# Half-width maximum products in an attention loop: one of three maxima per key tile made of 256 keys in each row half of TensorE, both in one PSUM bank

## The chip, the cores and the metric

The kernel runs on one core of a Trainium2 chip. Its engines are TensorE (PE, with its weight loads as PEld), VectorE (DVE), ScalarE (ACT), GpSimd (POOL) and SyncE (SP, which issues most DMAs). Each engine has its own instruction stream; semaphores order them. The metric is the device time of one execution in microseconds (us), as a median of several runs.

## The reference

One transformer block over 2048 tokens of width 640: attention with 32 heads of width 20, then a gated feed-forward network (FFN) of width 1728, each with a residual and a layer norm ahead of it.

```
h  = x + softmax(q k^T / sqrt(20)) v @ wo     (q, k, v from layernorm(x) @ wqkv)
h2 = h + (silu(z @ w_gate) * (z @ w_up)) @ w_down     (z = layernorm(h))
```

The softmax is exact in the sense that the row maximum is subtracted before the exponential. For each query the kernel therefore needs the maximum of its 2048 scores before the exponentials of that query begin.

## The kernel before, in words

**Stages.** First come the layer norm and the projections to queries, keys and values, beside which the first row maxima are found (`max_four`, L230). Then comes the attention loop (L1375). Then the output projection and the FFN follow.

**Units and key tiles.** The 32 heads are 8 groups of 4 heads. A unit `u` is one group with one chunk of 512 queries, so there are `NU` = 32 units. A unit is worked in `NT` = 16 key tiles of 128 keys, 512 key tiles in all. For one key tile the loop issues:

- four score products (`scores`, L1295), one for each head: 128 keys against 512 queries into one PSUM bank, followed by the exponential on ScalarE (L1306) from that bank to `probs`;
- one weighing of the key tile two earlier (`weigh`, L1308): four products with `values`, one for each head, each on 32 columns of TensorE, all 128 rows. The operands are plain fp32, and the trace shows each as two passes, eight matmuls in all;
- three maximum products for units that come later (`max_one`, L268): 128 queries against 512 keys into one bank, followed by a maximum over the 512 on VectorE (L280) into one slot of the small tile `mx` of that unit;
- and small pieces: a part of the preparation of FFN weights, loads of queries, the output of finished units (`row_sums` L1318, with one copy on ScalarE for each unit, L1320).

**Row halves.** The contraction of a score or maximum product has 60 or 62 rows only, so TensorE holds two of them at once: rows 0 to 63 (`b` = 0) serve two of the four heads and rows 64 to 127 (`b` = 1) the other two. Below, a small letter is a product in half 0, a capital one in half 1.

**Order.** It is written by hand. `ORDER` (L41) has one string for even and one for odd key tiles; `W` is the weighing with the small pieces, `s` and `S` are scores, `m` and `M` are maximum products:

```
ORDER = ("WsSmmSsM", "WSsMMsSm")
```

So one half gets four products of 512 columns and the other three, in turn. `singles` holds the list of maximum products for each half, and `next_max` (L1356) takes the next one of a half. When all maxima of a unit are there, `max_all` (L284) takes the maximum over its slots, and `max_parts`, `max_turn`, `max_load` or `max_finish` put the negated maximum into two extra rows of that unit's queries. There are 1472 such products of one half and 512 keys; at three a tile they last for some 491 of the 512 tiles, after which the order is `sSsSW`.

**PSUM.** Of the eight banks, four go round the scores (`ps_one`, L952), three go round the maximum products (`ps_max`, L959), and one holds the weighing's sum (`acc`). A product whose bank is still being read waits at its weight load.

Of the kernel before, what the change touches and what calls it, by code (L numbers as in the profile page):

```python
# [9 lines left out]
F32 = mybir.dt.float32  # L10
# [4 lines left out]
ALU = mybir.AluOpType  # L15
AX = mybir.AxisListType

P = 128
S = 2048
D = 640  # L20
H = 32
# [4 lines left out]
CH = 512  # L26
NC = S // CH
TPC = CH // P
# [9 lines left out]
LOWEST = -3.4028234e38  # L38
GD = G * DH

ORDER = ("WsSmmSsM", "WSsMMsSm")  # L41


@with_exitstack
def tile_block(ctx: ExitStack, tc: tile.TileContext, x, wqkv, wo, wg, wu, wd, out):
    nc = tc.nc
# [100 lines left out]
    NU = NG * NC  # L147
# [4 lines left out]
    stk = att_ctx.enter_context(tc.tile_pool(name="stk", bufs=1, side="right"))  # L152
    k_stk = [stay.tile([P, 2, S], F32R, name="k_stk0", tag="first")]
    v_stk = [stay.tile([P, NT, VG], F32, name="v_stk0", tag="second")]
    keys, queries, values = {}, {}, {}
# [24 lines left out]
    def load_keys(g, cs):  # L180

        k = keys[g] = k_stk[g % 2]
        stack(k[:, :, cs], 1, g, cs.start // CH)
# [11 lines left out]
        )  # L195

    def mx_tile(u, **tag):
        return stk.tile([P, 2, 2, TPC, NC], F32, name=f"mx{u}", **tag)

    mxs = {u: mx_tile(u) for u in range(NU) if u % NC < 2 or u == 2}  # L200

# [63 lines left out]

        return differences, maxima

    def max_one(u, kc, t, pair, b):  # L268

        ps = ps_max()  # L270
        if u not in mxs:
            mxs[u] = mx_tile(u, tag="mx_late", bufs=3)
        rows = slice(b * ROW, b * ROW + NPART)
        nc.tensor.matmul(  # L274
            ps,
            queries[u][rows, pair, t * P : (t + 1) * P],
            keys[u // NC][rows, pair, kc * CH : (kc + 1) * CH],
            start=True, stop=True,
        )
        nc.vector.tensor_reduce(  # L280
            mxs[u][:, b, pair, t, kc : kc + 1], ps, axis=AX.X, op=ALU.max
        )

    def max_all(u):  # L284

        ends[u] = stk.tile([P, G * TPC], F32, name="neg", tag="neg", bufs=2)
        nc.vector.tensor_reduce(
            ends[u], mxs[u].rearrange("p b h t k -> p (b h t) k"), axis=AX.X, op=ALU.max, negate=True
        )

    def max_parts(u):

        neg = ends[u]
        both = ends[u] = stk.tile([P, 2, G * TPC], F32R, name="neg2", bufs=2)
        nc.gpsimd.tensor_copy(both[:, 0], neg)
        nc.gpsimd.tensor_tensor(
            out=both[:, 1], in0=neg, in1=both[:, 0].bitcast(F32), op=ALU.subtract
        )
# [66 lines left out]
    with tc.tile_pool(name="pa", bufs=2) as pa:  # L365
# [21 lines left out]
        slot = [0]  # L387
# [468 lines left out]
        for c in range(NC):  # L856
# [7 lines left out]
            for j, (kind, *which) in enumerate(work):  # L864
# [31 lines left out]
                else:  # L896
# [10 lines left out]
                    def ps_max():  # L907
                        n = turn[0] % 5
                        turn[0] += 1
                        if n > 2:  # L910
                            return psum_two.tile([P, CH], F32, name="ps_max", tag="ps_two")
                        return psum.tile([P, CH], F32, name="ps_max", tag="ps_max", bufs=3)
# [4 lines left out]
                if (c, j) in ((1, 14), (1, 16), (2, 4), (3, 4)):  # L917
                    n = c if c > 1 else (j - 14) // 2
# [376 lines left out]
    def scores(u, kt, j, probs):  # L1295

        p, b = divmod(j, 2)
        rows = slice(b * ROW, b * ROW + NPART + 2)
        ps = ps_one()
        nc.tensor.matmul(  # L1300
            ps,
            keys[u // NC][rows, p, kt * P : (kt + 1) * P],
            queries[u][rows, p, :],
            start=True, stop=True,
        )
        nc.scalar.activation(probs[p][:, b, :], ps, AF.Exp, scale=scale)  # L1306
# [43 lines left out]
            )  # L1350

    todo, tail, accs, later, full, now = [], [], {}, {}, [], [0]
    singles = [[(*a, b) for a in rest] for b in range(2)]
    left = {u: sum(2 for a in rest if a[0] == u) for u in range(1, NU)}

    def next_max(b):  # L1356
        if singles[b]:
            a = singles[b].pop(0)
            max_one(*a)
            left[a[0]] -= 1  # L1360
            if left[a[0]] == 0:
                full.append(a[0])

    def weigh_next():
        u, kt, probs = todo.pop(0)
        if kt == 0:
            accs[u] = psum.tile([P, CH], F32, name="acc", tag=f"ps_{last % 3}")
        weigh(u, kt, probs, accs[u])
        if kt == NT - 1:
            queues = [nc.sync] if u + 1 < NU else [nc.scalar, nc.sync]  # L1370
            tail.append((u, *row_sums(accs.pop(u), *queues)))

    extra = []
    preparing = prepare_weights()
    for u in range(NU):  # L1375
        g, c = divmod(u, NC)
        if g == NG - 1 and c >= 2:
            _, first, ln, flips, _ = ahead
            extra = [*first, *ln, lambda: None, *flips]
        for kt in range(NT):  # L1380
            now[0] = u * NT + kt
            probs = [pp.tile([P, 2, CH], F32, name="probs") for _ in range(2)]
            heads = [[0, 2], [1, 3]]
            order = ORDER[now[0] % 2] if singles[0] or singles[1] else "sSsSW"
            for op in order:
                if op in "mM":
                    next_max(int(op == "M"))
                elif op in "sS":
                    scores(u, kt, heads[op == "S"].pop(0), probs)
                else:  # L1390
                    if len(todo) == 2:
                        weigh_next()
                    for f in later.pop(now[0], ()):
                        f()
                    if extra:
                        extra.pop(0)()
                    if preparing and u and kt not in (3, 4):
                        preparing.pop(0)()
                    if now[0] == (NU - NC) * NT + 8:
                        unit_ring, last_ring = weight_rings()  # L1400
                        unit_ring.fill()
# [51 lines left out]
    u, o, r = tail.pop()  # L1453
# [561 lines left out]
```

## Time and profile before

| what | value |
|---|---|
| median of 3 runs | 2027.66 us (2025.42 to 2028.07) |
| the profiled execution, its own time | 2025.84 us |
| its span, first to last instruction | 2024.0 us |
| granted TensorE clock, mean | 0.999 |
| first and last score product start | 319.2 and 1455.2 us |
| first and last maximum (L280) start | 321.2 and 1391.6 us |

The profile is of one execution. Busy time of an engine counts its instructions from their recorded start to their recorded end; on TensorE and ScalarE one instruction's end overlaps the next one's start, so the distance from start to start says what one costs in a stream, and the recorded duration says when its result is there. The line numbers are those of the kernel before. A weight load on PEld is listed with the line of its matmul.

### The profile page before, as it was taken

How to read it: one execution, taken by the hardware profiler on the slowest of the kernel's cores; microseconds unless marked ns; L12 is line 12 of the kernel's file. 1: busy time of each engine (PE TensorE's matmuls, PEld its weight loads, DVE VectorE, ACT ScalarE, POOL GpSimd, SP SyncE). 2: the span in 40 equal slices, each digit the busy share in tenths (PEclk: the TensorE clock that was granted, in tenths of full speed). 3: DMA queues.
4: the chain of work that ended last, by engine and by line, in shares of the span. 5: the costliest groups of instructions: out<-in, count | busy, mean ns of one | idle time of the engine just before them, and what ended most of it. 6: DMA issues, size and time to landing. Idle time of an engine off the chain costs nothing. (4 is left out here: it accounts for less than half of the span.)

```text
span 2024.0 us, 39916 instructions
## 1 busy us (share of the span) xinstructions
PE 2003.7 (99%) x14302; PEld 1242.0 (61%) x14302; DVE 1602.4 (79%) x2816; ACT 1439.9 (71%) x2827; POOL 788.5 (39%) x1166
## 2 busy tenths in 40 slices
PE   8999999999999999999999999999999999999999
PEld 6999995333334333333333333345588888888888
DVE  5687778888888898988988988875387666676677
ACT  4678878999999999999999999987633222212221
POOL 7464423334443453443400011011155444744555
PEclk9999999999999999999999999999999999999999
DMA  7877563443634544435412132221258654974642
GB/s 245 255 254 261 180 207 83 117 146 95 189 104 139 153 143 128 155 128 173 148 58 68 36 85 58 80 63 56 59 182 296 218 189 154 353 268 159 204 150 95
DMA packets 199340, 310.35 MB, mean 153 GB/s; under 512 B 53744, under 2 KB 87856, under 8 KB 198120
## 3 DMA queue, kind: packets, MB, share of 16 engines
q1 hardware_dynamic: 192552, 284.21, 43.7%
q0 software_dynamic: 6496, 23.60, 3.9%
q8 instruction: 114, 1.87, 0.4%
q14 instruction: 82, 0.67, 0.1%
q10 hardware_dynamic: 96, 0.00, 0.0%
HBM read 208.11 MB, written 99.19 MB: 152 GB/s over the span
## 5 line engine op out<-in xcount | busy, mean ns | idle before, releaser
L1306 ACT ACTIVATE probs<-ps_one 128x512 f32<-128x512 f32 x2048 | 1056.6, 615 | 61.2 <-PE ps_one L1300 35.3
L280 DVE TENSOR_REDUCE mx<-ps_max 128x1 f32<-128x512 f32 x1472 | 924.9, 684 | 106.3 <-PE ps_one L1300 77.6
L1300 PE MATMUL ps_one<-q_stk,k_stk 62*128 62x512 f32 x2048 | 583.3, 450 | 0.7 <-DMA q_stk<-m_d 0.6
L1310 PE MATMUL acc<-probs,v_stk 128*32 128x512 f32 x4096 | 546.2, 606 | 0.0
L1300 PEld LDWEIGHTS ps_one<-q_stk,k_stk 62*128 62x128 f32 x2048 | 248.7, 184 | 441.2 <-ACT probs L1306 416.7
L274 PE MATMUL ps_max<-k_stk,q_stk 60*128 60x512 f32 x1472 | 374.9, 426 | 1.0 <-DVE mx L261 0.9
L274 PEld LDWEIGHTS ps_max<-k_stk,q_stk 60*128 60x128 f32 x1472 | 272.8, 186 | 26.9 <-DVE mx L280 2.1
L1693 DVE TENSOR_TENSOR tmp<-ps_a,tmp 128x512 f32<-128x512 f32 x208 | 141.2, 689 | 122.4 <-PE ps_a L1478 96.7
L261 DVE TENSOR_REDUCE mx<-ps_max 128x2 f32<-128x512 f32 x288 | 180.7, 685 | 63.9 <-PE ps_max L239 58.7
L1310 PEld LDWEIGHTS acc<-probs,v_stk 128*32 128x32 f32 x4096 | 80.6, 108 | 179.0 <-issue 168.0
L251 ACT ACTIVATE ps_max<-ps_max 128x512 f32<-128x512 f32 x288 | 151.6, 584 | 42.9 <-PE ps_max L239 40.3
L1572 PE MATMUL ps_b<-halves,yp 128*128 128x320 f32 x1032 | 179.0, 308 | 1.5 <-DMA halves<-j_d 1.2
L1572 PEld LDWEIGHTS ps_b<-halves,yp 128*128 128x128 f32 x1032 | 165.2, 188 | 17.5 <-POOL yp L90 1.5
L1478 PE MATMUL ps_a<-t,units 128*128 128x512 f32 x624 | 162.5, 396 | 0.0
L90 POOL TENSOR_TENSOR yp<-y,yp 128x256 fp32r<-128x256 f32 x96 | 60.2, 627 | 189.8 <-ACT yp L89 189.8
L1478 PE MATMUL ps_a<-z,units 128*128 128x512 f32 x516 | 133.9, 394 | 0.0
L1478 PEld LDWEIGHTS ps_a<-t,units 128*128 128x128 f32 x624 | 112.6, 188 | 18.5
L1345 POOL TENSOR_TENSOR o<-o,rb 128x512 f32<-128x512 f32 x31 | 39.9, 1286 | 199.1 <-DMA q_stk<-q_d 74.1
L1577 DVE TENSOR_TENSOR h<-ps_b,h 128x320 f32<-128x320 f32 x248 | 109.9, 480 | 6.9 <-PE ps_b L1572 5.4
L643 PE MATMUL ps_one<-z_hi,w_lo 64*128 64x512 f32 x380 | 113.5, 392 | 0.0
L643 PE MATMUL ps_one<-z_lo,w_hi 64*128 64x512 f32 x380 | 112.3, 392 | 0.0
L643 PE MATMUL ps_one<-z_hi,w_hi 64*128 64x512 f32 x380 | 111.7, 393 | 0.0
(225 smaller groups left out, 2637.4 us busy)
## 6 DMA issues: line engine op xcount, KB each, us to landing
units<-w_d SPq DMA_DIRECT2D x186, 256.0 KB
w_d<-stage SPq DMA_DIRECT2D x106, 256.0 KB
halves<-j_d SPq DMA_DIRECT2D x70, 320.0 KB
j_d<-stage SPq DMA_DIRECT2D x42, 320.0 KB
k_stk<-k_d SPq DMA_DIRECT2D x64, 160.0 KB
q_stk<-q_d SPq DMA_DIRECT2D x64, 160.0 KB
raw<-k_d SPq DMA_DIRECT2D x62, 160.0 KB
raw<-q_d SPq DMA_DIRECT2D x54, 160.0 KB
```

Source lines behind the costliest of these rows:

```text
L251: nc.scalar.activation(ps, ps, AF.Relu)
L261: nc.vector.tensor_reduce(mx[:, b, :, t, kc], ps.rearrange("p (j n) -> p j n", j=2), axis=AX.X, op=ALU.max,)
L274: nc.tensor.matmul(ps, queries[u][rows, pair, t * P : (t + 1) * P], keys[u // NC][rows, pair, kc * CH : (kc + 1) * CH], start=True, stop=True,
L280: nc.vector.tensor_reduce(mxs[u][:, b, pair, t, kc : kc + 1], ps, axis=AX.X, op=ALU.max)
L643: nc.tensor.matmul(ps, a[rows], b[rows], start=(i == n == 0), stop=(i == 1 and n == last), skip_group_check=True,)
L1300: nc.tensor.matmul(ps, keys[u // NC][rows, p, kt * P : (kt + 1) * P], queries[u][rows, p, :], start=True, stop=True,)
L1306: nc.scalar.activation(probs[p][:, b, :], ps, AF.Exp, scale=scale)
L1310: nc.tensor.matmul(acc[32 * j : 32 * j + 32, :], values[u // NC][:, kt, j * VW : j * VW + 32], probs[j // 2][:, j % 2, :], start=(kt == 0) ...
L1478: nc.tensor.matmul(ps.rearrange("p (t n) -> p t n", t=TPC), w[k][:, i], z[k][:, :, j], start=(first and m == 0), stop=(last and m == len(n ...
L1572: nc.tensor.matmul(ps, a, b, start=(n == 0), stop=(n == len(pairs) - 1))
L1577: nc.vector.tensor_tensor(out=h, in0=ps, in1=h, op=ALU.add)
L1693: add = lambda out, ps, x: nc.vector.tensor_tensor(out=out, in0=ps, in1=x, op=ALU.add)
```

## The change

The three maximum products of a key tile are divided in another way. Each tile now has one in half 0 (`m`), one in half 1 (`M`), and one that is made of two products of 256 keys, one in each half (`h` and `H`), which write the two halves of one bank. One maximum on VectorE then reads that bank and writes two values, the maxima of two heads over the same 256 keys. Every key tile has the same order. The two halves of the array may not write one bank at the same time, so ahead of `H` stands a no-operation on TensorE that touches the bank and thereby waits for `h`.

Two such tiles cover the 512 keys of both heads, so the list of work (`rest`) is used up at the same rate as before. A maximum over 256 keys for the second part needs a slot of its own: `mx` gets two more slots, filled with the lowest number in advance (on GpSimd for tiles that exist from the start, on VectorE for the late ones), and `max_all` reduces over six slots where it reduced over four.

```diff
-ORDER = ("WsSmmSsM", "WSsMMsSm")
+ORDER, LAST_ORDER = "WhSmsSHMs", "sSsSW"
...
     def mx_tile(u, **tag):
-        return stk.tile([P, 2, 2, TPC, NC], F32, name=f"mx{u}", **tag)
+        n = NC + (2 if tag else u > 0)
+        return stk.tile([P, 2, 2, TPC, n], F32, name=f"mx{u}", **tag)
...
+    def max_slots(u):
+
+        if u not in mxs:
+            mxs[u] = mx_tile(u, tag="mx_late", bufs=3)
+            nc.vector.memset(mxs[u][:, :, :, :, NC:], LOWEST)
+        return mxs[u]
...
+    def max_half(ps, i, u, kc, t, pair, b):
+
+        k0 = kc * CH + i * (CH // 2)
+        cols = slice(b * CH // 2, (b + 1) * CH // 2)
+        max_product(ps[:, cols], u, t, pair, b, k0, k0 + CH // 2)
+
+    def max_halves(ps, i, u, kc, t, pair):
+
+        slot = kc
+        if i:
+            n = halved[u, t, pair] = halved.get((u, t, pair), 0) + 1
+            slot = NC - 1 + n
+            assert slot < max_slots(u).shape[-1]
         nc.vector.tensor_reduce(
-            mxs[u][:, b, pair, t, kc : kc + 1], ps, axis=AX.X, op=ALU.max
+            max_slots(u)[:, :, pair, t, slot], ps.rearrange("p (j n) -> p j n", j=2),
+            axis=AX.X, op=ALU.max,
         )
...
     def next_max(b):
-        if singles[b]:
-            a = singles[b].pop(0)
+        if not whole and rest:
+            a = rest.pop(0)
+            whole.extend((*a, i) for i in (b, 1 - b))
+        if whole:
+            a = whole.pop(0)
             max_one(*a)
-            left[a[0]] -= 1
-            if left[a[0]] == 0:
-                full.append(a[0])
+            counted(a[0], 1)
+
+    def next_half(b):
+
+        if not halves_of and rest:
+            a = rest.pop(0)
+            halves_of.extend((i, a, []) for i in range(2))
+        if not halves_of:
+            return
+        i, a, banks = halves_of[0]
+        if not banks:
+            banks.append(ps_max())
+            max_half(banks[0], i, *a, b)
+        else:
+            nc.tensor.keepalive_nop([nc.tensor.lower_ap(banks[0])])
+            max_half(banks[0], i, *a, b)
+            max_halves(banks[0], i, *a)
+            counted(a[0], 2 * i)
+            halves_of.pop(0)
...
+    for u in range(1, NU):
+        if u in mxs:
+            nc.gpsimd.memset(mxs[u][:, :, :, :, NC:], LOWEST)
...
-            order = ORDER[now[0] % 2] if singles[0] or singles[1] else "sSsSW"
-            for op in order:
+            for op in ORDER if rest or whole or halves_of else LAST_ORDER:
                 if op in "mM":
                     next_max(int(op == "M"))
+                elif op in "hH":
+                    next_half(int(op == "H"))
```

`max_product` holds the matmul that `max_one` had. The stages ahead of the attention loop and behind it are as they were.

More of the change, by code (lines that the diff above doesn't have):

```diff
@@ L266, in max_four, with max_product @@
         return differences, maxima
[L268 to L272, printed above, removed]
+    def max_product(ps, u, t, pair, b, k0, k1):
         rows = slice(b * ROW, b * ROW + NPART)
@@ L276, in max_one @@
             queries[u][rows, pair, t * P : (t + 1) * P],
-            keys[u // NC][rows, pair, kc * CH : (kc + 1) * CH],
-            start=True, stop=True,
-        )
+            keys[u // NC][rows, pair, k0:k1],
+            start=True, stop=True, skip_group_check=True,
+        )
+    halved = {}
+    def max_slots(u):
[3 more added lines that the diff above has]
+        return mxs[u]
+    def max_one(u, kc, t, pair, b):
+        ps, mx = ps_max(), max_slots(u)
+        max_product(ps, u, t, pair, b, kc * CH, (kc + 1) * CH)
+        nc.vector.tensor_reduce(mx[:, b, pair, t, kc : kc + 1], ps, axis=AX.X, op=ALU.max)
+    def max_half(ps, i, u, kc, t, pair, b):
[8 more added lines that the diff above has]
+            assert slot < max_slots(u).shape[-1]
         nc.vector.tensor_reduce(
-            mxs[u][:, b, pair, t, kc : kc + 1], ps, axis=AX.X, op=ALU.max
+            max_slots(u)[:, :, pair, t, slot], ps.rearrange("p (j n) -> p j n", j=2),
+            axis=AX.X, op=ALU.max,
         )
@@ L1352, in tile_block, with counted @@
     todo, tail, accs, later, full, now = [], [], {}, {}, [], [0]
-    singles = [[(*a, b) for a in rest] for b in range(2)]
     left = {u: sum(2 for a in rest if a[0] == u) for u in range(1, NU)}
-    def next_max(b):
-        if singles[b]:
-            a = singles[b].pop(0)
-            max_one(*a)
-            left[a[0]] -= 1
-            if left[a[0]] == 0:
-                full.append(a[0])
+    whole, halves_of = [], []
+    def counted(u, n):
+        left[u] -= n
+        if n and left[u] == 0:
+            full.append(u)
+    def next_max(b):
+        if not whole and rest:
[3 more added lines that the diff above has]
+            a = whole.pop(0)
+            max_one(*a)
+            counted(a[0], 1)
[15 more added lines that the diff above has]
+            halves_of.pop(0)
     def weigh_next():
```

## The prediction, on record before the changed kernel ran

> **What bounds the kernel now.** I read the busy shares first, then the windows of the attention loop, then single key tiles in the timeline.
>
> ```profile
> PE 2003.7 (99%) x14302; PEld 1242.0 (61%) x14302; DVE 1602.4 (79%) x2816; ACT 1439.9 (71%) x2827; POOL 788.5 (39%) x1166
> 400.00:600.00 200.00, 200.00 (x1408) 78.37 (x1405) 179.30 (x301) 194.78 (x383) 86.95 (x163) 1.00 0.43 133
> 1000.00:1200.00 200.00, 200.00 (x1407) 78.11 (x1404) 179.41 (x300) 195.11 (x383) 19.43 (x28) 1.00 0.21 59
> PEld ps_one L1300 <- ACT probs L1306: 416.7, 529, 1.6
> ```
>
> The window columns are PE, PEld, DVE, ACT and POOL, then the clock. PE is busy all the time, ACT 97%, DVE 90%; the wait list even says that score weights wait for the exponential. Busy shares do not decide between PE and ACT here, because recorded durations overlap. Starts do. Two key tiles on PE, and ACT in three places:
>
> ```profile
> 901.09 1.06 PE L1310 MATMUL acc<-probs,v_stk 128*32 128x512 f32 x8
> 902.09 0.50 PE L1300 MATMUL ps_one<-q_stk,k_stk 62*128 62x512 f32 x2
> 902.43 0.39 PE L274 MATMUL ps_max<-k_stk,q_stk 60*128 60x512 f32 x1
> 902.43 0.39 PE L1300 MATMUL ps_one<-q_stk,k_stk 62*128 62x512 f32 x1
> 902.66 0.51 PE L274 MATMUL ps_max<-k_stk,q_stk 60*128 60x512 f32 x2
> 902.89 0.40 PE L1300 MATMUL ps_one<-q_stk,k_stk 62*128 62x512 f32 x1
> 904.22 0.50 PE L1300 MATMUL ps_one<-q_stk,k_stk 62*128 62x512 f32 x2
> 904.55 0.39 PE L274 MATMUL ps_max<-k_stk,q_stk 60*128 60x512 f32 x1
> 904.56 0.39 PE L1300 MATMUL ps_one<-q_stk,k_stk 62*128 62x512 f32 x1
> 904.78 0.51 PE L274 MATMUL ps_max<-k_stk,q_stk 60*128 60x512 f32 x2
> 905.02 0.40 PE L1300 MATMUL ps_one<-q_stk,k_stk 62*128 62x512 f32 x1
> 905.34 1.06 PE L1310 MATMUL acc<-probs,v_stk 128*32 128x512 f32 x8
> 906.34 0.50 PE L1300 MATMUL ps_one<-q_stk,k_stk 62*128 62x512 f32 x2
> 902.62 0.60 ACT L1306 ACTIVATE probs<-ps_one 128x512 f32<-128x512 f32 x1
> 904.07 0.62 ACT L1306 ACTIVATE probs<-ps_one 128x512 f32<-128x512 f32 x1
> 905.50 0.66 ACT L1306 ACTIVATE probs<-ps_one 128x512 f32<-128x512 f32 x1
> 907.41 0.71 ACT L1306 ACTIVATE probs<-ps_one 128x512 f32<-128x512 f32 x1
> ```
>
> A tile takes 2.13 us (902.09 to 904.22). On PE it is a closed chain of starts. The weighing to the first score pair is 1.00 (901.09 to 902.09, and 905.34 to 906.34). That pair costs 0.34, since its weights load with nothing beside them. Two slots of 0.23 follow. The last product to the next weighing is 0.32 (905.02 to 905.34). The sum is 1.00 + 0.34 + 0.23 + 0.23 + 0.32 = 2.12, the tile but for rounding. ACT has room: from 905.50 to 907.41 lie four steps of an unbroken run, 0.48 each, so four exponentials need 1.91. PE bounds the loop.
>
> The last of the four slots shows what is wasted. One score product stands alone there, with half of the array idle, because one half has four products and the other three.
>
> The rows also show that **the halves run ahead of each other**. Written as `sSmmSsM` (or its mirror), a strict order would give: a score pair, one maximum product alone, the second maximum product with a score, a score with the third maximum product. The trace has, behind the pair, a maximum product with a score (902.43), two maximum products together (x2 at 902.66, and again at 904.78) and a score alone. So the score written behind the second maximum product started ahead of it, and the product written last started ahead of the score before it. Each half takes its own products as they come.
>
> **The change, part by part.**
>
> *The slots.* Half 0 now gets `h m s s`, half 1 gets `S S H M`: three and a half products of 512 columns each, where it was four against three.
>
> ```profile
> 303.66 0.39 PE L643 MATMUL ps_one<-z_hi,w_hi 64*128 64x512 f32 x1
> 303.88 0.51 PE L239 MATMUL ps_max<-raw 60*128 60x256 f32 x4
> 304.13 0.39 PE L643 MATMUL ps_one<-z_hi,w_hi 64*128 64x512 f32 x1
> L239 PE MATMUL ps_max<-raw,raw 60*128 60x256 f32 x608 | 81.1, 287 | 0.2
> ```
>
> In the stage before, four products of 256 columns in row halves, two in each half, take 0.25 us (303.88 to 304.13): 0.12 each in a half, with weights. So in half 0 of the new tile `h` ends at 0.23 (0.34 less 0.23, plus 0.12), then come three products of 0.23, the last one from 0.69. In half 1 the scores run to 0.57, `H` to 0.69 and `M` from there. The weighing starts 0.32 later, at 1.01, where it was at 1.13. **PE alone: 2.13 - 0.12 = 2.01 us**, with 490.7 tiles (1472 / 3) some 57 us.
>
> *The added matmul and weight load* are inside the 0.12. *The maximum* keeps its price: two outputs from 512 inputs cost VectorE what one does.
>
> ```profile
> L280 DVE TENSOR_REDUCE mx<-ps_max 128x1 f32<-128x512 f32 x1472 | 924.9, 684 | 106.3 <-PE ps_one L1300 77.6
> L261 DVE TENSOR_REDUCE mx<-ps_max 128x2 f32<-128x512 f32 x288 | 180.7, 685 | 63.9 <-PE ps_max L239 58.7
> 902.85 1.89 DVE L280 TENSOR_REDUCE mx<-ps_max 128x1 f32<-128x512 f32 x3 [0.24 <-PE ps_one L1300]
> ```
>
> Three in a run take 1.89, or 0.60 a step and 1.81 a tile: under 2.01, so DVE is not the bound. Its banks are held longer, though. `h` takes one of three banks at the tile's start. By these steps the maxima start at 0.66 (`m`: 0.23 + 0.39 + 0.04), 1.27 (`H`) and 1.87 (`M`, done at 2.55). The next `h` needs `H`'s bank at 2.0, free at 1.95; the next `M` loads its weights at 2.6, free at 2.6. Nothing is left over, so each late maximum is paid by PE.
>
> *The wait on itself.* The trace has no such wait. What is queued behind it: `H`, `M`, the last score and the next weighing, and with them ScalarE's fourth exponential and two maxima. `h` starts with the tile; as a first product it ends at 0.11 + 0.28 = 0.39.
>
> ```profile
> 905.98 0.67 ACT L1306 ACTIVATE probs<-ps_one 128x512 f32<-128x512 f32 x1
> 906.70 0.18 PEld L1300 LDWEIGHTS ps_one<-q_stk,k_stk 62*128 62x128 f32 x1
> L274 PEldq EVENT_SEMAPHORE  x66: 51/51/320, 365.0 to 1324.9; - x66
> ```
>
> From an awaited end (905.98 + 0.67 = 906.65) to the weights behind it is 0.05; a separate wait instruction on PE's queue lasts 0.05 when it is already met. So the wait passes at 0.44 to 0.49, `H`'s weights take 0.11, and `H` could start at 0.55 to 0.60 where its half is free at 0.57. Lower end: nothing, hidden under `S`. Upper end: the wait covers everything issued before it, and 0.33 us a tile is lost (below). I take nothing, the value that the rows give.
>
> *What is late next.* Four banks go round the scores, so the fourth score needs the fourth exponential of the tile before.
>
> ```profile
> 904.54 0.63 ACT L1320 ACTIVATE o<-acc 128x512 f32<-128x512 f32 x1
> 908.62 0.73 PE L1300 MATMUL ps_one<-q_stk,k_stk 62*128 62x512 f32 x3
> ```
>
> That exponential ends 2.60 us after its tile's start (904.07 + 0.62 - 902.09). Add 0.05 for the wait, 0.11 for weights, 0.32 to the weighing and 1.00 to the next pair: 4.08 us for two tiles, so **a tile can't be under 2.04**. That is above PE's 2.01, and I take it: 2.13 - 2.04 = 0.09 less a tile, 490.7 x 0.09 = 44 us.
>
> With the slack gone, the copy that ScalarE makes once a unit (0.48 in a run) costs more. Today the tile behind it takes 2.28 (906.34 to 908.62), 0.15 more. Then ScalarE's idle time in a tile is 2.04 + 0.53 - 1.98 - 0.48 = 0.11 (first exponential 0.53 after the pair, fourth 1.98), and the copy delays the fourth score by 0.48 - 0.11 = 0.37. That is 0.22 more in each of 30 units, 7 us back.
>
> *Slots and fills.* Two more slots make 96 inputs of 64 in `max_all`, by its row
>
> ```profile
> L287 DVE TENSOR_REDUCE neg<-mx x30: 207/215/222, 344.4 to 1327.0; 128x16 f32<-128x64 f32 x30
> ```
>
> at most half as much again, 0.1 us x 30 = 3 us on DVE if nothing hid it. The fills are 32 elements each. DVE's spare 0.2 a tile hides most; I take 2 us for both and for banks held longer where the output projection shares them.
>
> **Sum.** 44 - 7 - 2 = 35 us. The profiled execution took 2025.84, 1.8 under the median: 2025.84 - 35 = 1990.8, as a median **1992.7 us**.
>
> **The rivals.**
>
> 1. *ScalarE's loop does not bind*, the score's bank comes free sooner than I count: PE's 2.01, and the copy's stall as now, 490.7 x 0.12 = 57 us less, 1971. For it: 0.03 us a tile separates the two. Chance 0.15.
>
> 2. *Nothing is gained, since products start in the order written.* Then the second `S` cannot start before the `s` ahead of it, at 0.46; `H` comes at 0.69, `M` and the last score at 0.81, the weighing at 1.13 as now: 2028, give or take 3. Against it stand the two maximum products in one slot. Chance 0.08. It includes a self-wait that is dropped in building with no other effect of the order.
> The Trainium skill, "TensorE: Matmul & The Clock Gate", Part 3 (The mechanism), has this as a rule: matmuls are "pc-monotone in start AND end". By that rule the sum would be 0 us in place of 35. The starts at 902.66 and 904.78 do not agree with it, so it keeps only this chance.
>
> 3. *Slower: the self-wait passes only when all products before it are done.* The semaphore may count the scores between as well. The second `s` starts at 0.46 and ends at 0.85, the wait passes at 0.90, `H` starts at 1.01, `M` at 1.13, the weighing at 1.45: a tile of 2.45, or 0.32 x 490.7 = 157 us more, 2185. It decides once the wait passes later than 0.57 after the tile's start, since then `M` starts later than 0.80, where the fourth slot starts now. For it: no trace shows a wait of PE on itself. Against it: `h` is the oldest product in the queue, and the wait names its bank. Chance 0.15.
>
> **How the numbers follow.** The forecast (1980 to 2010) has 0.62. A difference under 0.2%, some 4 us, is about what a measurement of this kernel can't tell from none. Faster by more: 0.62 + 0.15 = 0.77. Same: 0.08. Slower: 0.15. The range from 1968 to 2032 takes in the first two rivals and leaves out the third with a few in a hundred below; between forecast and 2032 lie waits that are partly hidden and late maxima.
>
> **What would show it.** Right: in the timeline a tile of 2.03 to 2.06 us, `m` 0.23 after `h`, two products in flight in all slots, no wait instruction of PE that ends past 0.5 us in the tile, exponentials almost without gaps, and the weighing's distance to the next pair still 1.00. The weights of the fourth score then wait for L1306. The stages before 319 and behind the last score keep their lengths. Wrong: the score behind the two maxima starting in order; `H` later than 0.6 in the tile; weights of `h` or `M` waiting for DVE in most tiles; or a gain under 15 us with PE still without gaps, which would mean that the half product costs more than 0.12.

## The result, and the profile after

The changed kernel takes **2012.84 us** (2012.53 to 2015.11, 4 runs) where the kernel before took 2027.87 (2025.42 to 2029.81, 4 runs): ratio 0.9937, 95% interval 0.9925 to 0.995. By the medians it is 15 us faster, by the ratio, which is not the medians' quotient, some 13; the forecast was 35 us. The profiled execution has a span of 2010.4 us where it was 2024.0, so 13.6 us are there to be accounted for.

In this profile the score product is L1328, its exponential L1334, the maximum product L272, the maximum over 512 L292, the maximum over two halves L307, the weighing L1338, the copy L1348 and the no-operation L1411. From its page, the busy times and the groups of VectorE's two kinds of maximum:

```profile
PE 1985.1 (99%) x14794; PEld 1268.7 (63%) x14794; DVE 1599.5 (80%) x2831; ACT 1440.1 (72%) x2827; POOL 789.4 (39%) x1182
L292 DVE TENSOR_REDUCE mx<-ps_max 128x1 f32<-128x512 f32 x980 | 671.8, 686 | 90.6 <-PE ps_max L272 88.0
L307 DVE TENSOR_REDUCE mx<-ps_max 128x2 f32<-128x512 f32 x492 | 335.8, 683 | 0.4 <-PE ps_max L272 0.4
```

492 of 1472 maxima now write two values and take the same time, 683 ns against 686. TensorE has 492 matmuls more. Its busy share stays at 99%, which again says nothing about what it waits for. The window of the loop, with the columns as before (PE, PEld, DVE, ACT, POOL, clock):

```profile
1000.00:1200.00 200.00, 200.00 (x1533) 84.74 (x1529) 182.70 (x307) 198.87 (x390) 16.81 (x24) 1.00 0.22 59
```

A tile has 16 matmuls now and had 15: 1533 / 16 = 95.8 tiles in 200 us, 2.09 us each with all stalls in it, where 1407 / 15 = 93.8 gave 2.13. One tile on PE by start, and behind it some of its weight loads:

```profile
890.27 0.38 PE L272 MATMUL ps_max<-k_stk,q_stk 60*128 60x256 f32 x1
890.27 0.50 PE L1328 MATMUL ps_one<-q_stk,k_stk 62*128 62x512 f32 x1
890.49 0.39 PE L272 MATMUL ps_max<-k_stk,q_stk 60*128 60x512 f32 x1
890.61 0.51 PE L1328 MATMUL ps_one<-q_stk,k_stk 62*128 62x512 f32 x2
890.84 0.34 PE L272 MATMUL ps_max<-k_stk,q_stk 60*128 60x256 f32 x1
890.96 0.40 PE L1328 MATMUL ps_one<-q_stk,k_stk 62*128 62x512 f32 x1
891.02 0.39 PE L272 MATMUL ps_max<-k_stk,q_stk 60*128 60x512 f32 x1
891.34 1.07 PE L1338 MATMUL acc<-probs,v_stk 128*32 128x512 f32 x8
892.33 0.38 PE L272 MATMUL ps_max<-k_stk,q_stk 60*128 60x256 f32 x1
```

```profile
890.26 0.18 PEld L272 LDWEIGHTS ps_max<-k_stk,q_stk 60*128 60x128 f32 x1 [0.84 <-DVE mx L307]
...
890.80 0.18 PEld L272 LDWEIGHTS ps_max<-k_stk,q_stk 60*128 60x128 f32 x1
890.85 0.18 PEld L1328 LDWEIGHTS ps_one<-q_stk,k_stk 62*128 62x128 f32 x1
890.90 0.19 PEld L272 LDWEIGHTS ps_max<-k_stk,q_stk 60*128 60x128 f32 x1
```

The tile takes 2.07 us (890.27 to 892.33, rounded). `h` and the first score start together, and `m` follows at 0.22. `H` is the maximum product at 890.84. Its half was free at 0.57 (a pair, 0.34, and a score, 0.23), yet its weights load only from 0.53 (890.80), so that with 0.11 for them it starts at 0.64. (The record begins at 0.57, but is 0.06 longer than the 0.28 of a half product in a stream.) So `M` is at 0.75 (891.02) where the forecast had 0.69, and the weighing at 1.07 where it had 1.01; the 1.00 to the next pair holds. The wait in brackets on the first line is the change from the weighing to row halves that is there in every tile; it names a maximum over two halves that had ended 0.12 us before (889.46 + 0.68 = 890.14).

Between `h` and the weights of `H` lies the no-operation. All of them, and those of two tiles:

```profile
L1411 PEldq EVENT_SEMAPHORE  x492: 51/51/51, 320.3 to 1378.1; - x164
```

```profile
L1411 PEldq EVENT_SEMAPHORE  x2: 51/51/51, 890.7 to 892.8; - x2
```

In the trace the one at 890.7 starts 0.43 into the tile, 0.04 behind the end of `h` (0.38), and ends at 0.48. It raises a semaphore of its own, and the weights of `H` wait for that one: they start 0.05 later. **The wait has two steps**, `h` to no-operation and no-operation to `H`.

**The account of the 13.6 us**, from the distances between weighings in both traces (464 of them, and those behind; "others" are kinds of tile with under 1 us each):

| part | forecast | measured |
|---|---|---|
| the ordinary tile: 2.128 to 2.069 us, median (27.4 in 464 tiles), and those behind them (2.4) | +44 | +29.8 |
| the tile behind ScalarE's copy: 0.15 over the median to 0.31 | -7 | -3.7 |
| first tiles of units: wait for rows of maxima | 0 | -4.3 |
| tiles in which a reciprocal on VectorE waits for a DMA | 0 | -2.3 |
| half the clock for a moment at the loop's start | 0 | -1.5 |
| slots, fills, last pieces of a unit's maxima, others | -2 | -3.4 |
| before and behind the loop | 0 | -1.0 |
| sum (by parts, rounded) | +35 | +13.6 |

The row of half the clock belongs to these two executions and can't be put down to the change: e9 below issues the same products and has the full clock there, and the kernel before has half the clock from 1392.5 to 1395.9, where a tile takes 2.92 us that takes 1.95 in e8 (some 1 us of the 2.4 in the first row).

The copy can be read off the timelines of ScalarE and PE:

```profile
898.93 0.63 ACT L1348 ACTIVATE o<-acc 128x512 f32<-128x512 f32 x1
```

```profile
900.61 0.50 PE L1328 MATMUL ps_one<-q_stk,k_stk 62*128 62x512 f32 x1
900.83 0.39 PE L272 MATMUL ps_max<-k_stk,q_stk 60*128 60x512 f32 x1
901.06 0.51 PE L1328 MATMUL ps_one<-q_stk,k_stk 62*128 62x512 f32 x2
902.99 0.38 PE L272 MATMUL ps_max<-k_stk,q_stk 60*128 60x256 f32 x1
```

That tile takes 2.38 us. Its second pair of scores comes 0.45 after the first, not 0.34, and what follows is later still. The longest new stall is at the start of one unit, on SyncE's queue and then on PE:

```profile
690.85 2.82 SPq L354 DMA_DIRECT2D q_stk<-m  x4
```

```profile
693.38 0.38 PE L272 MATMUL ps_max<-k_stk,q_stk 60*128 60x256 f32 x1
694.96 0.47 PE L1328 MATMUL ps_one<-q_stk,k_stk 62*128 62x512 f32 x1 [1.20 <-DMA q_stk<-m]
```

Four DMAs bring a unit's negated maxima into its queries; issuing them takes 2.82 us on the queue. The last maxima of such a unit are counted only with the second half product of a piece, a tile later than before (171 tiles into the loop, not 170). That spare tile had been the cover. The list of waits names the reciprocal's cause too:

```profile
DVE r L1359 <- DMA r<-o: 2.6, 2, 1.6
PE ps_one L1328 <- DMA q_stk<-m: 1.8, 2, 1.2
PEld ps_max L272 <- PEq L1411: 2.0, 8, 0.3
```

The columns are total, times and longest. Its last line is instructive: the wait on itself, which by the experiments below costs over 12 us, has 2.0 us here, since half 0 goes on working meanwhile. Only the starts show it.

### The profile page after: what moved, and what is told of

The parts are those of the page before. It is cut to its first block, busy times and chain, and to the rows that moved or that the text cites. A ratio compares the mean times of both kernels' runs of the same rounds, so it can differ in the third digit from the quotient of the medians.

```text
span 2010.4 us, 41923 instructions
## 1 busy us (share of the span) xinstructions
PE 1985.1 (99%) x14794; PEld 1268.7 (63%) x14794; DVE 1599.5 (80%) x2831; ACT 1440.1 (72%) x2827; POOL 789.4 (39%) x1182
## 5 line engine op out<-in xcount | busy, mean ns | idle before, releaser
L1334 ACT ACTIVATE probs<-ps_one 128x512 f32<-128x512 f32 x2048 | 1056.1, 612 | 46.7 <-PE ps_one L1328 37.2
L292 DVE TENSOR_REDUCE mx<-ps_max 128x1 f32<-128x512 f32 x980 | 671.8, 686 | 90.6 <-PE ps_max L272 88.0
L272 PEld LDWEIGHTS ps_max<-k_stk,q_stk 60*128 60x128 f32 x1964 | 294.2, 185 | 462.8 <-DVE mx L307 393.5
L1328 PE MATMUL ps_one<-q_stk,k_stk 62*128 62x512 f32 x2048 | 570.4, 427 | 2.7 <-DMA q_stk<-m 1.8
L272 PE MATMUL ps_max<-k_stk,q_stk 60*128 60x256 f32 (+1 forms) x1964 | 565.5, 376 | 2.5 <-DVE mx L292 1.2
L1338 PE MATMUL acc<-probs,v_stk 128*32 128x512 f32 x4096 | 546.1, 605 | 0.1
L307 DVE TENSOR_REDUCE mx<-ps_max 128x2 f32<-128x512 f32 x492 | 335.8, 683 | 0.4 <-PE ps_max L272 0.4
L1328 PEld LDWEIGHTS ps_one<-q_stk,k_stk 62*128 62x128 f32 x2048 | 304.9, 184 | 15.0 <-ACT probs L1334 11.3
L262 DVE TENSOR_REDUCE mx<-ps_max 128x2 f32<-128x512 f32 x288 | 180.8, 685 | 63.7 <-PE ps_max L240 60.2
L1338 PEld LDWEIGHTS acc<-probs,v_stk 128*32 128x32 f32 x4096 | 80.7, 108 | 128.1 <-issue 119.9
```

Of the source, the lines that this page charges most:

```text
L262: nc.vector.tensor_reduce(mx[:, b, :, t, kc], ps.rearrange("p (j n) -> p j n", j=2), axis=AX.X, op=ALU.max,)
L272: nc.tensor.matmul(ps, queries[u][rows, pair, t * P : (t + 1) * P], keys[u // NC][rows, pair, k0:k1], start=True, stop=True, skip_group_ch ...
L292: nc.vector.tensor_reduce(mx[:, b, pair, t, kc : kc + 1], ps, axis=AX.X, op=ALU.max)
L307: nc.vector.tensor_reduce(max_slots(u)[:, :, pair, t, slot], ps.rearrange("p (j n) -> p j n", j=2), axis=AX.X, op=ALU.max,)
L1328: nc.tensor.matmul(ps, keys[u // NC][rows, p, kt * P : (kt + 1) * P], queries[u][rows, p, :], start=True, stop=True,)
L1338: nc.tensor.matmul(acc[32 * j : 32 * j + 32, :], values[u // NC][:, kt, j * VW : j * VW + 32], probs[j // 2][:, j % 2, :], start=(kt == 0) ...
```

## The experiments

The theory (A): the second step makes `H` 0.06 late, and this alone holds the tile above the 2.04 of ScalarE's loop. The rivals are that the half product costs more than 0.12, or that ScalarE's loop itself is longer than counted. Further theories concern the copy (C) and the rows of maxima (E). Times are medians; ratios are to the kernel before on the same chip (2025.64 us for the first four, 2024.93 for the next four, 2024.63 for the following three, 2025.31 for the last two).

**e1: the wait doubled.**

```diff
-            nc.tensor.keepalive_nop([nc.tensor.lower_ap(banks[0])])
+            for _ in range(2):
+                nc.tensor.keepalive_nop([nc.tensor.lower_ap(banks[0])])
```

> The no-operation ahead of H is issued twice. In the changed kernel's trace the wait is two steps: a wait instruction lasts 0.05 us and is itself waited for by the weights of H, which start 0.05 behind its end, so H starts 0.64 us into its tile where its row half is free at 0.57. Theory A (the wait in front of H, two steps long, is what ends the tile): one more such instruction puts 0.05 us on every one of 490.7 tiles, a tile of 2.12, and the time is near 2037 us. Rival B (the wait is hidden and ScalarE's loop over the four score banks, or VectorE, sets 2.07): no change, 2013 us within 3.

Measured: 2077.44 us, ratio 1.0254 (1.0237 to 1.0272); the median tile is 2.223. The weight loads of one tile, whose first starts at 900.76, and the list of waits:

```profile
900.76 0.18 PEld L272 LDWEIGHTS ps_max<-k_stk,q_stk 60*128 60x128 f32 x1 [0.84 <-DVE mx L307]
...
901.45 0.18 PEld L272 LDWEIGHTS ps_max<-k_stk,q_stk 60*128 60x128 f32 x1 [0.27 <-PEq L1412]
...
902.98 0.18 PEld L272 LDWEIGHTS ps_max<-k_stk,q_stk 60*128 60x128 f32 x1 [0.84 <-DVE mx L307]
```

```profile
PEld ps_max L272 <- PEq L1412: 138.8, 488, 0.5
```

The weights of `H` load 0.68 into the tile, where it was 0.53, and the tile grows by as much, 0.154. So what is added between `h` and `H` lies on the path, all of it: A is right in kind. The size was missed. The second no-operation waits for the semaphore that the first raised and starts 0.10 behind its end, so that each further one costs 0.15 and not its 0.05. With it the wait is visible in the list, 138.8 us in 488 tiles.

**e2, e3, e4: the work on one side or the other made shorter.** e2 takes half of `h` away (the wait is then over sooner), e3 an eighth of each exponential, e4 both.

```diff
-        max_product(ps[:, cols], u, t, pair, b, k0, k0 + CH // 2)
+        n = CH // 2 if b else 128
+        max_product(ps[:, cols][:, :n], u, t, pair, b, k0, k0 + n)
...
-        nc.scalar.activation(probs[p][:, b, :], ps, AF.Exp, scale=scale)
+        nc.scalar.activation(probs[p][:, b, :448], ps[:, :448], AF.Exp, scale=scale)
```

> The product h takes 128 keys where it took 256, so it ends 0.05 us earlier and its row half has no more to do; the maximum still reads the whole bank, whose other 128 columns hold old values, so half of the keys of h are left out of the maxima. The three banks of the maxima are held as fixed tiles. Theory A: the wait passes 0.05 us earlier, H starts at 0.585, M at 0.70, and the next limit is ScalarE's loop at 2.04: a tile of 2.04, 490.7 x 0.026 = 13 us less, 2000 us. Rival B (ScalarE's loop or VectorE sets 2.07 already): 2013 us within 3.

> The exponentials take 448 of their 512 columns; the other 64 of each probs tile stay at one, so they are left out of the result. The probs tiles are held as six fixed tiles, set once on GpSimd. Each exponential is then some 0.06 us shorter. Theory A: the ordinary tile stays at 2.07, since H ends it and not ScalarE; only the stall behind ScalarE's copy, 0.31 us once a unit, shrinks to 0.1 or less: 6 to 9 us less, 2004 to 2007. Rival B (ScalarE's loop sets the tile): the ordinary tile falls to 2.01 to 2.03, 20 to 30 us less beside the copy, about 1980.

> Both edits of the two kernels before: h of 128 keys and exponentials of 448 columns, with the same parts left out. Theory A with ScalarE's loop as the second limit, at 2.04 us a tile: with both gone TensorE alone is left, 2.01 us a tile, 490.7 x 0.055 = 27 us and 8 us of copies less: about 1978 us. If VectorE's banks or something else were the second limit, the tile would stay near 2.04 and the time near 1992.

| | time | ratio (95% interval) | median tile |
|---|---|---|---|
| e2 | 2009.67 | 0.9917 (0.9903 to 0.9932) | 2.043 |
| e3 | 2020.1 | 0.9973 (0.9956 to 0.9991) | 2.075 |
| e4 | 1992.96 | 0.9835 (0.9819 to 0.985) | 2.014 |

A tile of e2, and two tile starts of e4 with the rows between:

```profile
891.39 0.32 PE L272 MATMUL ps_max<-k_stk,q_stk 60*128 60x128 f32 x1
...
891.98 0.28 PE L272 MATMUL ps_max<-k_stk,q_stk 60*128 60x256 f32 x1
892.07 0.44 PE L1334 MATMUL ps_one<-q_stk,k_stk 62*128 62x512 f32 x1
892.09 0.40 PE L272 MATMUL ps_max<-k_stk,q_stk 60*128 60x512 f32 x1
892.44 1.06 PE L1344 MATMUL acc<-probs,v_stk 128*32 128x512 f32 x8
```

```profile
891.94 0.32 PE L272 MATMUL ps_max<-k_stk,q_stk 60*128 60x128 f32 x1
...
892.52 0.28 PE L272 MATMUL ps_max<-k_stk,q_stk 60*128 60x256 f32 x1
892.62 0.39 PE L1334 MATMUL ps_one<-q_stk,k_stk 62*128 62x512 f32 x1
892.65 0.40 PE L272 MATMUL ps_max<-k_stk,q_stk 60*128 60x512 f32 x1
892.97 1.06 PE L1344 MATMUL acc<-probs,v_stk 128*32 128x512 f32 x8
893.97 0.32 PE L272 MATMUL ps_max<-k_stk,q_stk 60*128 60x128 f32 x1
```

The three tiles separate three limits. With the wait over sooner `H` runs as soon as its half is free (0.59 after the start, in 0.28), and the tile falls to **2.043**: ScalarE's loop, forecast 2.04. Now the fourth score is the late one: its record is longer (0.44, not 0.39) than in e4, where it isn't, and in the median tile its weights load 0.052 behind the end of the exponential that frees its bank (0.198 in e4). In the changed kernel that distance is 0.051 already: the fourth score waits for ScalarE there too, but it starts at 0.69 and `M` at 0.75, and `M` ends the tile. So it is `H` that matters in e2, and not that half 0 has 0.06 less to do. With shorter exponentials alone the ordinary tile gets no shorter (2.075), so that loop does not bind the changed kernel. With both the tile is **2.014**: PE alone, forecast 2.01, so the half product `H` does cost 0.12.

The totals were missed. In e2 and e4 the loop's first weighing is at 326.98 and 326.57, where it was at 323.33: they use fixed tiles for the maxima's banks or the exponentials, which are filled first (e12, which holds the banks without filling them, is at 323.2). Beside that the stalls at the first tiles of units grow to 6.2 and 9.8 us, and the loop's last 47 tiles with all that follows take 4.5 and 2.6 us more. In e3 the tiles behind the copy lose nothing any more (7.9 us in the changed kernel), as was expected. But it starts as late, and nine tiles that lost next to nothing lose 0.8 to 2.0 us each, 11 us in all. In four of them TensorE stops for 0.7 to 1.0 us with nothing shown that it waits for, and goes on 1.3 to 1.5 us after a DMA packet of the kind "instruction" has landed. Instructions that come late are a likely cause, but no run tests it.

**e5: the copy made shorter**, 128 columns of 512.

```diff
-        nc.scalar.activation(o, acc, AF.Copy)
+        nc.scalar.activation(o[:, :P], acc[:, :P], AF.Copy)
```

> The copy that ScalarE makes once a unit takes 128 of its 512 columns (the other columns of the two o tiles, which are fixed here, stay at one, so three quarters of the attention output are left out). Theory C: the tile with the copy takes 2.38 us where the others take 2.07 because ScalarE has 0.14 us to spare in a tile and the copy takes 0.48; with a quarter of it the stall goes, 29 x 0.3 = 8 us less, 2004 to 2006 us. Rival D: that tile waits for the weighing's bank or for a DMA of the unit's end, whatever the copy's length: 2013 us within 3.

Measured: 2002.39 us, ratio 0.9886 (0.9873 to 0.99). The ordinary tile stays at 2.067; the tiles behind the copy lose 0.4 us in all where they lost 7.9. C holds: the copy's length is what these tiles wait for, and ScalarE has no room for it.

**e6, e7: the rows of maxima a tile sooner**; in e7 the reciprocals a tile later too.

```diff
-                    later.setdefault(now[0] + 2, []).append(lambda v=v: max_finish(v))
+                    sooner_rows.setdefault(now[0] + 1, []).append(lambda v=v: max_finish(v))
...
-                    later.setdefault(now[0] + 4, []).append(lambda v=v: max_turn(v))
-                    later.setdefault(now[0] + 6, []).append(lambda v=v: max_load(v))
+                    later.setdefault(now[0] + 3, []).append(lambda v=v: max_turn(v))
+                    later.setdefault(now[0] + 5, []).append(lambda v=v: max_load(v))
...
-            if kt == (3 if sooner else 4) and tail:
+            if kt == (3 if sooner else 5) and tail:
```

> The rows of maxima are made one key tile earlier: max_finish at the end of the key tile behind the one that completes a unit's maxima where it stood in the next tile's weighing, max_turn and max_load one tile earlier each. Nothing else is changed. Theory E: in the changed kernel the maxima of every fourth unit are complete one key tile later (tile 171 where it was 170, for a unit that starts at 176), the four DMAs of their rows are issued at 690.85 to 693.67 and the unit's first scores, due at 693.4, wait for them; first tiles of units lose 5.1 us in all where they lost 0.8. One tile sooner takes away most of it: 3 to 4.5 us less, 2008.5 to 2010 us. Rival F: the DMA queue or GpSimd makes them late and not the tile in which they are issued: 2013 us within 1.5.

> The same as the kernel with the rows one tile earlier, and the reciprocals of the unit before, which block VectorE until a DMA lands, at key tile 5 of a unit where they stood at 4. The tile behind them lost 2.2 us in two units and VectorE's order costs some 0.5 more in others. Theory: 2 us less than the kernel with the earlier rows, 2006.5 to 2008 us. Rival: the DMA that they wait for is late by more than a tile, or its wait moves to GpSimd's product: the same as that kernel.

Measured: e6 2008.93 us, ratio 0.9924 (0.991 to 0.9937); e7 2013.28, 0.9939 (0.9926 to 0.9951). In e6 the first tiles lose 2.5 us where they lost 5.1, and the span falls by 4.0, mostly as E has it (the reciprocals' tiles lose 1.3 less as well); the ratios' intervals overlap with that of the change, so the gain stands on the trace. In e7 the reciprocals' stall is gone (2.2 to 0.04), but the stall at the first tiles is back (4.9). Here is where it waits, by the list of waits of e7:

```profile
PE ps_one L1328 <- DMA q_stk<-m: 3.0, 3, 1.3
```

A stall removed in one place came back in another, and why was not traced; the miss is the assumption that the gains add.

**e8: the slots and fills alone**, with the order of before and its way of taking the products from the list.

```diff
-ORDER, LAST_ORDER = "WhSmsSHMs", "sSsSW"
+ORDER, LAST_ORDER = ("WsSmmSsM", "WSsMMsSm"), "sSsSW"
```

> The order and the products of the kernel before, three maximum products of 512 keys a tile, in alternating halves, with what else the change brought: six slots, their fills, and a maximum over 96 inputs once a unit. Theory: these cost 2 us or less, since VectorE has 0.3 us to spare in a tile of 2.13: 2026 to 2030 us. Rival G: they are what eats the gain (10 us or more of the stalls): 2036 us or more.

Measured: 2026.93 us, ratio 1.0013 (1.0004 to 1.0022), some 2.6 us of cost; the tile is 2.131. They are not where the missing gain went. Its loop begins with the same moment at half the clock as the changed kernel's, so that needs no half products.

**e9, e10, e11: one step instead of two.** In e9 the no-operation touches only the columns that `h` writes; e10 adds e6's edit, and e11 divides the copy.

```diff
-            nc.tensor.keepalive_nop([nc.tensor.lower_ap(banks[0])])
+            nc.tensor.keepalive_nop([nc.tensor.lower_ap(banks[0][:, : CH // 2])])
...
-        nc.scalar.activation(o, acc, AF.Copy)
+        nc.scalar.activation(o[:, :320], acc[:, :320], AF.Copy)
+        nc.vector.tensor_copy(o[:, 320:], acc[:, 320:])
```

> Nothing of the computation is left out; the no-operation ahead of H touches the 256 columns that h writes and no longer H's own half of the bank. Theory A (what the wait costs is its second step: H's weights wait for the end of the no-operation, and not only for the end of h): with nothing of its own left to wait for, H's weights go behind the no-operation in the queue, H starts at about 0.58 in the tile where it started at 0.64, the tile falls to the 2.04 that ScalarE's loop of four banks sets, and the time to 2013 - 13 = 2000, give or take 4. Rival D (the second step is there whatever the no-operation touches, because the two products share a bank, or the weights load no sooner after a wait that is passed in the queue): tile 2.07 and 2013, give or take 3. Which it is can be read from the weights of H: whether they still wait for the semaphore that the no-operation raises, and where they start.

> Nothing is left out: e9's no-operation, and the rows of maxima one key tile sooner as in e6. The two act on different tiles (all of them; the first tiles of units), so theories A and E together: the gain of e9 plus 4, so 1996 if e9 takes 2000, and e6's 2009 if e9 brings nothing. Rival F (the stall only moves to the next wait once the tile is shorter, as with the reciprocals in e7): no better than e9 by more than 1.

> Nothing is left out: e10, and the copy that ScalarE makes once a unit is divided, 320 columns on ScalarE and 192 on VectorE. Theory C (the copy's length on ScalarE is what the tile behind it waits for; e5 took 384 columns away and 8 us went): 192 / 384 of 8, so 4 us less than e10, if VectorE, which has about 0.2 a tile to spare, takes the 192 columns in that. Rival H (VectorE's part costs as much, since the maxima behind it hold their banks longer): e10's time, give or take 2.

Measured: e9 2013.97 us, ratio 0.9944 (0.9931 to 0.9957), tile 2.069; e10 2010.58, 0.9933 (0.9919 to 0.9947); e11 2011.89, 0.9939 (0.9926 to 0.9952). In e9 a tile starts at 890.59 and `H` loads its weights here:

```profile
891.12 0.18 PEld L272 LDWEIGHTS ps_max<-k_stk,q_stk 60*128 60x128 f32 x1
```

That is at 0.53 again, and in the trace these weights still wait for the no-operation's semaphore. The edit did not remove the second step, so it tests nothing about A: rival D's outcome. Its loop begins at the full clock. e10 is e6 again. In e11 ScalarE's part did get shorter, and VectorE's part waits for it:

```profile
L1349 DVE COPY o<-acc 128x192 f32<-128x192 f32 x32 | 11.4, 358 | 15.1 <-ACT o L1348 14.3 <-issue 0.7
```

The copy tiles lose 4.1 us, not 7.4 as in e10, but VectorE stands idle for 14.3 us before its parts and does not go on with the maxima behind them, and the tiles ahead lose 5.6 where they lost 0.2. That is rival H's time, by this wait and not by the banks that H names.

**e12, e13: `H` due later**, behind `M`, with the banks going round so that the next `h` finds a free one; e13 adds e6's edit.

```diff
-ORDER, LAST_ORDER = "WhSmsSHMs", "sSsSW"
+ORDER, LAST_ORDER = "WhSmsSMHs", "sSsSW"
...
+    held_max = [psum.tile([P, CH], F32, name="ps_max", tag="ps_max", bufs=3) for _ in range(3)]
+
     def ps_max():
-        return psum.tile([P, CH], F32, name="ps_max", tag="ps_max", bufs=3)
+        held_max.append(held_max.pop(0))
+        return held_max[-1]
...
         if not banks:
+            ps_max()
             banks.append(ps_max())
```

> Nothing is left out. In half 1 the whole product M comes ahead of the half product H (order WhSmsSMHs in place of WhSmsSHMs), and the three banks of the maxima go round by one each tile, so that the next h takes the bank that is read out first and not H's. Theory A (H starts in the tile 0.06 late because the wait on itself has two steps; that alone holds the tile at 2.07): M is at 0.57, H is due only at 0.80, and the wait, passed with both steps at 0.53, lies beside the second score and M; the tile falls to ScalarE's 2.04, and the time to 2013 - 13 = 2000, give or take 4. Rival J (a no-operation on the queue costs its 0.03 wherever it stands, for the loads behind it come late): 2.07 and 2013. Rival K (the maximum over two halves ends later and its bank is missing for the third product of the tile behind): weights of L272 wait for DVE in most tiles, 2.1 or more, 2025 or more.

> Nothing is left out: e12, and the rows of maxima one key tile sooner as in e6. By theories A and E 4 less than e12, so 1996 if e12 takes 2000. Rival F (with a shorter tile the stall only moves to another wait): e12's time, give or take 2.

Measured: e12 2033.35 us (2025.88 to 2040.41), ratio 1.0039 (1.0026 to 1.0053); e13 2034.45, 1.006 (1.0038 to 1.0082): slower than both kernels. Tile starts on PE in e12, then the weight load of `M` in the first of these tiles, the maximum of two halves ahead of it on VectorE, and a start of TensorE at another place:

```profile
891.22 0.38 PE L272 MATMUL ps_max<-k_stk,q_stk 60*128 60x256 f32 x1
...
893.25 0.38 PE L272 MATMUL ps_max<-k_stk,q_stk 60*128 60x256 f32 x1
...
895.34 0.38 PE L272 MATMUL ps_max<-k_stk,q_stk 60*128 60x256 f32 x1
```

```profile
891.71 0.18 PEld L272 LDWEIGHTS ps_max<-k_stk,q_stk 60*128 60x128 f32 x1
```

```profile
890.98 0.68 DVE L307 TENSOR_REDUCE mx<-ps_max 128x2 f32<-128x512 f32 x1
```

```profile
621.15 0.58 PE L272 MATMUL ps_max<-k_stk,q_stk 60*128 60x256 f32 x1 [1.60 <-issue]
```

Tiles alternate, 2.03 and 2.09 here. The weights of `M` load 0.05 behind the end of the maximum over two halves of the tile before (890.98 + 0.68 = 891.66, then 891.71), since `M` now takes `H`'s bank: rival K's mechanism. One tile in two loses the time again that the wait no longer costs, and a pair of tiles takes 4.12 us, as two tiles of the change do. That a tile of 2.03 exists with the no-operation in it speaks against rival J, but A's gain did not come. With its ordinary tiles as long as the change's, e12 is slower by what lies elsewhere, so that rival K's "2025 or more" came out by luck. TensorE stops four times, for 1.6 to 2.6 us (up to 489.2, 621.1, 1000.7 and 1214.9), with nothing shown that it waits for, and goes on 1.4 to 1.6 us after a packet of instructions has landed, as in e3. At the last three the granted clock goes to 0.50, for 14 us in all. Together with the tile behind them these stops cost some 15 us of the 23 by which the span is longer than the changed kernel's. Another 6 us lie in the loop's last tiles, which share their banks with the output projection and take 5.5 us each where they took 4.5; there the projection's weights wait for the maximum of two halves (10.1 us, 7 times).

A direct wait of `H` on `h`, with nothing on the queue between them, wasn't tried. No version of these that computes everything is shown to beat the change by more than the intervals; e6 is the best of them.

## Why the prediction was wrong in size

**The step that failed** is the wait on itself: "`H` could start at 0.55 to 0.60 where its half is free at 0.57 ... I take nothing". The pieces were right one by one: an awaited end counts 0.04 to 0.05 later, and the instruction lasts 0.05. Their sum left out a piece, the second handing over: in the trace `h` ends at 0.383, the no-operation starts 0.043 later and lasts 0.051, the weights start 0.054 later and take 0.105: 0.64. The prediction added an end and an instruction, and let the weights follow the instruction at once. Of the 0.06, 0.03 would have been hidden by ScalarE's 2.04; the rest, 2.069 - 2.043 = 0.026 in 490 tiles, is 13 us of the missing 20. The Trainium skill, "Perfetto Trace Analysis", Per-instruction lifecycle, says that the time in which a semaphore's update becomes visible lies outside the window that a profile shows for an instruction. The rows fit that: 0.05 lies between the no-operation's recorded end and the weights, and e1 has 0.10 between two no-operations.

**The next 8 us** are new waits at few tiles, which the prediction did not look for, at the units whose rows of maxima come a tile later (4.3) and at the reciprocals (2.3), and the moment at half clock (1.5), which e9 does without. It priced instructions that moved inside a tile, not what the later completion of a unit's maxima moves: each DMA that `max_finish` and `max_load` issue, on SyncE's queue.

**What held.** The half product `H` costs 0.12 (e4, 2.014 against 2.01). ScalarE's loop is 2.04 (e2, 2.043). Shorter exponentials alone do nothing for the ordinary tile as long as the wait binds (e3). The copy's stall was 0.37 in the forecast and is 0.31 in the trace; e5 shows its cause. Slots and fills: 2 forecast, some 2.6 by e8. The two maxima in one take 683 ns as forecast. Of the signs that the prediction named for its being wrong, "`H` later than 0.6 in the tile" is what the trace has (0.64). The reading that it gave to a small gain without gaps on TensorE, a half product dearer than 0.12, is not borne out by e4.

**The rivals.** ScalarE's loop does bind once the wait is shorter (e2), so 1971 was out of reach. "Products start in the order written" would have given no gain; in the tile at 890.27 the score written last starts at 890.96, ahead of `M`, written before it, at 891.02. That the wait covers all products before it (2185) did not come true: it passes 0.04 behind the end of `h`, while scores written before it are still running. That rival's point of decision, a wait that passes later than 0.57, was not reached: the no-operation ends at 0.48 and `M` starts at 0.75, before 0.80, so the tile did not become longer than it was. `H` came 0.06 late instead of 0.44 (1.01 less 0.57).

## What to carry to other kernels

A wait of an engine on its own earlier work is a chain: price the end, the waiting instruction, and the handing on to what it protects, each with the gap behind it, and compare the sum with the moment at which the protected instruction is due. If a half of the engine keeps working, a list of waits can hide most of the price (it had 2.0 us of 13 here); two starts show it. When an edit moves the last piece of a batch by one step, follow everything that waits for the batch to be complete, DMA issues above all, before calling it free; and a stall that is moved out of one tile (e7, e11, e12) has to be looked for in the next.

## What the runs showed of the hardware that was not expected

- A semaphore wait on TensorE's queue with an instruction of 0.051 us: 0.04 from the end of the awaited matmul to its start, 0.05 from its end to the weights behind it. Each further one in the chain adds 0.15 (e1).
- TensorE can stop with nothing shown that it waits for. All 14 such stops of over 0.4 us in the loops of e3, e12 and e13 end 1.3 to 1.6 us after a DMA packet of the kind "instruction" has landed; the other kernels have none.
- For a moment at the loop's start the granted clock is 0.50 in the changed kernel's execution, where the kernel before has 1.00. A window of each:

```profile
324.00:325.00 1.00, 1.00 (x8) 0.00 (x0) 0.58 (x1) 0.59 (x2) 1.00 (x1) 0.50 0.99 313
```

```profile
324.00:325.00 1.00, 1.00 (x10) 0.30 (x4) 0.91 (x2) 0.40 (x1) 1.00 (x1) 1.00 0.91 215
```

The clock is the third column from the end. e8, which has the products of before, shows it too, and e9, which has the products of the change, does not. Inside the traces such stretches last 3.4 us (the changed kernel, e8), 6.8 (e2, e3, e10) or 10.2 (e4). What sets them off stays open.
